# V loaded ahead, scale and router chains in parts, V split on GpSimd: a clustered attention feeding two MLP stages

## The chip, the cores and the metric

The kernel runs on one core of a Trainium2 chip (trn2). The metric is the device time of one execution in microseconds (us). An execution is one launch that computes the whole reference. The engines are TensorE (PE, with PEld for its weight loads), VectorE (DVE), ScalarE (ACT), GpSimd (POOL) and SyncE (SP), whose queue issues most DMAs. Each engine works through its own queue in order.

## What is computed

Attention with a cluster mask, then a mixture of experts with one expert per token, then a gated MLP:

```python
# q, k, v: (2, 8, 768, 64); centroids: (8, 16, 64)
q_assign = argmax(q_n . c_n); k_assign = argmax(k_n . c_n)   # nearest of 16 centroids
scores = scale * (q @ k^T), -1e9 where q_assign != k_assign
attn = exp(scores - max); attn /= sum
x = (attn @ v), heads side by side                            # (1536, 512)
e_idx = argmax(x @ w_gate)                                    # one of 8 experts
out[mask_e] = gate_w * eom * (relu(x[mask_e] @ w1[e]) @ w2[e])   # w1 512x1024
h = out @ w_in; return (h * sigmoid(h)) @ w_out               # 512x2048, 2048x512
```

All inputs are f32 and the result is f32.

## The kernel before

**Attention** takes the first 320 us or so. It goes through 2 batches x 8 heads in 8 pairs of heads, numbered 0 to 7; a pair has 12 steps, one for each 128-row tile of each of its two heads, 96 steps in all. In step i the loop `run` writes, in this order: the scores of step i+1 on TensorE (`qk_mm`, L367 and L369), the softmax of step i (`soft`: on VectorE the minimum L388, since the scores are held negated, on ScalarE the exp L390 and a cast to f16 L399), the transposed probabilities of step i-1, and the product with V (`pv`, L458 to L460) for a step that lies some 7 back.

The probabilities are kept as two f16 parts, a high one and what is left over. Transposing them goes one of two ways. For two steps in every six, which `onpe` picks, TensorE transposes the f32 (L414), ScalarE copies the high part (L420) and VectorE subtracts the low part (L425). For the others the high part comes from ScalarE (L399) or, in steps 4, 5 and 8 of a pair, from VectorE (L433); GpSimd subtracts the low part (L434) and a DMA on SP's queue transposes two steps at once (L438). `due` says from which step on a product may run.

**V** is used as two f16 parts as well, scaled by a power of two per head. `load_v` is a generator: it loads the V of a batch (768 rows x 8 heads, two DMAs of 768 KB, L118), takes the largest absolute value in four reductions (L123), and then turns it on TensorE, computes the scale on 8x8 tiles on VectorE (L128 to L135), spreads it with a matmul (L137) and copies it (L139). `split_v` makes the two parts of one head, `vh` and `vl` (L151, L152), twice per pair. The pool `att_v` of V has one buffer, so the second V (`vt` of batch 1) can be loaded only when the last head of batch 0 has been split.

**What sets the order.** `plan` makes for each pair a list of small pieces of work with a rank r (step in the pair, -1 being the step before it): the loads, transposes and masks of the next pairs, the splits, and for pairs 0 and 3 the parts of `load_v`. `run` takes from the list what is due in each step. Beside it runs at most one part per step of the router's generator `rg` (`pair`, for the gate logits of a pair of heads, and after the last pair of a batch `route`, the whole chain of expert choice, ranks and slots L713 to L747 and six scatters L757 of the rows into expert order). At the end of the attention part every instruction gets a dependency on its predecessor on the same engine, so the order written is the order run there.

**The experts** start with a read of the scattered rows back (`xt<-xst`) and TensorE's transposes (`etp`, L890) at about 340 us, with weights loaded ahead on SP's queue; then comes the gated MLP. TensorE is nearly always busy from there to the end.

## Time and profile before

| | us |
|---|---|
| Median of 3 runs | 868.56 (866.24 to 875.82) |
| The profiled execution | 866.39 |
| Span of its trace | 864.5 |
| Attention, first exp of pair 0 to last exp | 25.19 to 311.00 |
| Tail to the first expert | 311.00 to 340.00 |
| TensorE busy over the span | 753.1 (87%) |
| VectorE busy | 531.9 (62%) |
| ScalarE busy | 416.6 (48%) |
| GpSimd busy | 293.5 (34%) |

The rows further down come from one execution. A row of the windows gives for a stretch its length, then for each engine the busy time and the number of instructions, TensorE's granted clock (1.00 is 2.4 GHz, 0.50 is 1.2 GHz), the mean share of the 16 DMA engines and the rate moved. A row of the timeline gives start, duration, engine, line, operation, output<-input with their shapes, the number of operations in the row, and in brackets how long the engine had stood idle before it and what ended that. A row on a line gives the number of its instructions, their shortest, median and longest duration in ns, and where in the span they lie.

### The profile page before, as it was taken

The numbers are of one execution on the slowest core, as the hardware profiler recorded it, in microseconds if no ns is written. First come the engines' busy times: TensorE is split into PE (matmuls) and PEld (weight loads), VectorE is DVE, ScalarE is ACT, GpSimd is POOL, SyncE is SP. The second block draws the span as 40 slices with busy tenths as digits, with TensorE's granted clock in tenths as the row PEclk, the third lists the DMA queues.
The fourth block names the chain that finished last, engine by engine and source line by source line (L and its number), as shares of the span: only waits on it lengthen the run. The fifth ranks groups of instructions, "written<-read, shape, count | busy, mean of one in ns | idle before, by whom it ended". The sixth has DMA issues, their size and how long they took to land.

```text
span 864.5 us, 14020 instructions
## 1 busy us (share of the span) xinstructions
PE 753.1 (87%) x5404; PEld 639.3 (74%) x5404; DVE 531.9 (62%) x933; ACT 416.6 (48%) x657; POOL 293.5 (34%) x225
## 2 busy tenths in 40 slices
PE   5859897698899873999999999879799999999994
PEld 4649876597788762987887897657588788878883
DVE  6687886868989867366654778599933322232221
ACT  3747775466677644465444655456522322222211
POOL 1665563436744305654342546254400000000000
PEclk9658998579899995999999999979999999999998
DMA  4399899576877737587664874565400100010001
GB/s 149 69 221 208 172 167 244 108 151 121 206 137 126 152 102 268 193 274 237 232 221 131 281 256 129 199 227 174 144 1 0 50 1 1 0 49 1 0 1 52
DMA packets 138856, 117.88 MB, mean 136 GB/s; under 512 B 103927, under 2 KB 110071, under 8 KB 138784
## 3 DMA queue, kind: packets, MB, share of 16 engines
q1 hardware_dynamic: 134832, 107.85, 46.5%
q0 software_dynamic: 3952, 9.08, 3.7%
q8 instruction: 44, 0.72, 0.3%
q14 instruction: 28, 0.23, 0.1%
HBM read 71.67 MB, written 18.45 MB: 104 GB/s over the span
## 4 chain that ended last, share of the span: by engine, by line
PE 33%; DVE 8%; issue 4%; DMA 4%; ACT 1%; POOL 0%; ACTq 0%; SPq 0%; DVEq 0%; POOLq 0%
PE op L1131 13%; PE hp L1143 12%; PE yp L950 4%; DVE stage L1076 2%; PE hp L933 2%; PE hr L915 2%; DVE stage L1075 2%; DMA x<-ys,f 1%; DVE stage L1077 1%; DMA stage<-in_moe_w 1%; DMA stage<-in_moe_w_in 1%; DVE GL L837 1%; DMA out_x<-os 0%; DVE w L837 0%; DVE sg L1151 0%
## 5 line engine op out<-in xcount | busy, mean ns | idle before, releaser
L837 POOL TENSOR_TENSOR w<-stage,w 128x512 fp32r<-128x512 f32 (+1 forms) x54 | 102.7, 1909 | 110.9 <-ACT w L832 101.6
L434 POOL TENSOR_TENSOR p<-p,p 128x768 f16<-128x768 f32 x62 | 105.1, 1706 | 98.8 <-ACT p L390 38.4
L1143 PE MATMUL hp<-XH,w 128*128 128x512 f32 x384 | 126.5, 403 | 8.6 <-DVE sg L1151 7.5
L832 ACT ACTIVATE w<-stage 128x1024 fp32r<-128x1024 f32 (+1 forms) x104 | 96.4, 940 | 57.9 <-DVE stage L1077 25.9
L390 ACT ACTIVATE p<-sp,m 128x768 f32<-128x768 f32 x96 | 86.4, 900 | 59.9 <-DVE m L388 55.4
L1131 PE MATMUL op<-w,GH 128*128 128x512 f32 x384 | 112.0, 397 | 0.0
L1151 DVE TENSOR_TENSOR sg<-hp,sg 128x512 f32<-128x512 f32 x48 | 33.1, 689 | 118.9 <-ACT sg L1150 118.9
L388 DVE TENSOR_REDUCE m<-sp 128x1 f32<-128x768 f32 x96 | 90.8, 951 | 22.8 <-PE sp L369 16.9
L933 PEld LDWEIGHTS hp<-X,w 128*128 128x128 f32 x672 | 87.2, 192 | 12.7 <-DVE HL L936 9.2
L933 PE MATMUL hp<-X,w 128*128 128x256 f32 x672 | 90.9, 285 | 5.7 <-DVE HL L936 5.5
L1143 PEld LDWEIGHTS hp<-XH,w 128*128 128x128 f32 x384 | 73.5, 192 | 28.1 <-DVE sg L1151 9.7
L1150 ACT ACTIVATE sg<-hp 128x512 f32<-128x512 f32 x48 | 28.5, 594 | 119.8 <-PE hp L1143 118.7
L1131 PEld LDWEIGHTS op<-w,GH 128*128 128x128 f32 x384 | 73.0, 190 | 17.2
L837 DVE TENSOR_TENSOR w<-stage,w 128x1024 fp32r<-128x1024 f32 x50 | 69.7, 1403 | 25.6 <-ACT w L832 25.3
L458 PE MATMUL o<-vh,pt 128*128 128x66 f16 x576 | 68.9, 204 | 16.5 <-DVE xb L467 11.1
L1143 PE MATMUL hp<-XL,w 128*128 128x512 f32 x192 | 77.5, 403 | 2.7 <-DVE XL L837 2.7
L367 PE MATMUL sp<-KA,QA 128*128 128x384 f32 x192 | 66.7, 432 | 13.7 <-ACT p L390 13.1
L458 PEld LDWEIGHTS <-pt 128*128 128x128 f16 x576 | 56.7, 103 | 20.7 <-issue 10.1
L1131 PE MATMUL op<-w,GL 128*128 128x512 f32 x192 | 67.1, 397 | 1.9 <-DVE GL L837 1.8
L459 PE MATMUL o<-vl,pt 128*128 128x64 f16 x576 | 68.2, 200 | 0.0
L460 PE MATMUL o<-vh,pt 128*128 128x66 f16 x576 | 67.9, 201 | 0.0
L950 PE MATMUL yp<-w,HH 128*128 128x512 f32 x224 | 63.4, 398 | 0.6 <-ACT HH L935 0.6
(205 smaller groups left out, 1442.4 us busy)
## 6 DMA issues: line engine op xcount, KB each, us to landing
stage<-in_moe_w SPq DMA_DIRECT2D x72, 512.0 KB, 4.7
stage<-in_moe_w_in SPq DMA_DIRECT2D x16, 512.0 KB, 4.7
stage<-in_moe_w_out SPq DMA_DIRECT2D x16, 512.0 KB, 3.5
xst<-z SPq DMA_DIRECT2D x16, 258.0 KB, 3.5
xt<-xst SPq DMA_DIRECT2D x7, 516.0 KB, 3.9
vt<-in_v SPq DMA_DIRECT2D x4, 768.0 KB, 7.1
xt<-x SPq DMA_DIRECT2D x6, 512.0 KB, 5.2
out_x<-os SPq DMA_DIRECT2D x12, 256.0 KB, 2.5
```

The lines of the kernel that those rows point to most:

```text
L388: st['min'] = nc.vector.tensor_reduce(m, sv, axis=AX.XY, op=ALU.min).ins
L390: st['exp'] = nc.scalar.activation(p32, sv, AF.Exp, bias=m, scale=-1.0).ins
L434: s.nc.gpsimd.tensor_sub(p16[:, 1], p32, p16[:, 0])
L458: nc.tensor.matmul(o[:, t, 0:D + 2], lhsT=pt[:, 0, kt], rhs=vh[:, kt], start=kt == 0, stop=False)
L459: nc.tensor.matmul(o[:, t, 0:D], lhsT=pt[:, 0, kt], rhs=vl[:, kt], start=False, stop=False)
L460: nc.tensor.matmul(o[:, t, 0:D + 2], lhsT=pt[:, 1, kt], rhs=vh[:, kt], start=False, stop=kt == NT - 1)
L832: s.nc.scalar.activation(hi, src, AF.Copy)
L837: (eng or s.nc.vector).tensor_sub(lo, src, hi)
L933: nc.tensor.matmul(hp, lhsT=W1[k][w][:, f * 128:(f + 1) * 128], rhs=x[:, k, :N], start=n == 0, stop=n == 11)
L950: nc.tensor.matmul(yp, lhsT=h[:, f, i * 128:(i + 1) * 128], rhs=w, start=n == 0, stop=n == 23)
L1131: nc.tensor.matmul(op[i], lhsT=g[:, i * 128:(i + 1) * 128], rhs=w, start=f == 0 and m == 0, stop=f == 15 and m == 2)
L1143: nc.tensor.matmul(hp, lhsT=I[k, f // 8][w][:, fs], rhs=x[:, k], start=n == 0, stop=n == 11)
```

## The change

Buffers: the pool of V goes from one buffer to two; the pool of masks goes from two to one and that of the f16 probabilities (`p16`) from four to three.

V of batch 1 is loaded in pair 1 at rank 3 instead of in pair 3 at rank 1. Its maxima stand in pairs 1 and 2, two in each; the transpose, VectorE's scale chain, the matmul and the copy are now four parts, at ranks 4, 5 and 6 of pair 3. The parts for V of batch 0 are spread the same way in pair 0.

The split is three GpSimd operations: the scaling in place, a cast, a subtraction.

`route` yields between its pieces, so that the chain is a part per step, and one scatter is a part; parts marked 'free' may also run in steps whose transposes are on TensorE.

The last twelve steps all have their transposes on TensorE (before, the last eight), their products may come three steps after and up to three in one step.

```diff
-        s.mkp = P('att_mk', 2)
+        s.mkp = P('att_mk', 1)
-        s.p16 = P('att_p16', 4)
+        s.p16 = P('att_p16', 3)
-        s.vp = P('att_v', 1)
+        s.vp = P('att_v', 2)
...
         nc.tensor.transpose(pb[0:8, 0:128], am, s.ident)
+        yield
         g = s.sm.tile([8, 1], F32, tag='vg', name='vg')
...
         nc.vector.tensor_scalar(dg[:, 0], s.ident[0:8, 0:8], rg, None, op0=ALU.mult)
+        yield
         pb2 = s.T('vps2')
         nc.tensor.matmul(pb2[:, 0:16], lhsT=s.one8, rhs=dg.rearrange('p a h -> p (a h)'), start=True, stop=True)
+        yield
...
-        nc.vector.tensor_scalar(vh[:, :, 0:D], src, sc[:, 0, h:h + 1], None, op0=ALU.mult)
-        nc.vector.scalar_tensor_tensor(vl, src, sc[:, 0, h:h + 1], vh[:, :, 0:D], op0=ALU.mult, op1=ALU.subtract)
+        nc.gpsimd.tensor_scalar(src, src, sc[:, 0, h:h + 1], None, op0=ALU.mult)
+        nc.gpsimd.tensor_copy(vh[:, :, 0:D], src)
+        nc.gpsimd.tensor_sub(vl, src, vh[:, :, 0:D])
...
-            for r in (4, 5, 6, 7, 8, 8):
+            for r in (3, 4, 4, 5, 6, 7, 8, 8):
                 add(r, nx(vg))
...
-        if pi == 3:
+        if pi == 1:
             s.v1 = s.load_v(1)
-            for r in (1, 4, 5, 6, 7, 9, 9):
-                add(r, nx(s.v1))
+        for r in {1: (3, 6, 10), 2: (6, 10), 3: (4, 5, 6, 6)}.get(pi, ()):
+            add(r, nx(s.v1))
...
-        return (g % 3 == 0 and g >= 6) or g >= n - 4
+        return (g % 3 == 0 and g >= 6) or g >= n - 6
...
-            for k in range(2):
+            for k in range(3 if i >= n - 12 else 2):
                 if done < min(n, i + 1) and i >= s.due(steps[done]):
...
-                if rg and (k == 0 or (i - base) % 12 == 9 and i < n - 12) and not (1 <= i < n + 1 and i < n - 9 and s.onpe(steps[i - 1])) and next(rg[0], 1):
-                    rg.pop(0)
+                if rg and (k == 0 or (i - base) % 12 == 9 and i < n - 12) and (free or not (1 <= i < n - 12 and s.onpe(steps[i - 1]))):
+                    x = next(rg[0], 0)
+                    free = x == 'free'
+                    if x == 0:
+                        rg.pop(0)
...
-            return i + 3 if i >= len(s.steps) - 8 else i + 7
+            return i + 3 if i >= len(s.steps) - 12 else i + 7
...
-            s.route(b, att, g)
+            for x in s.route(b, att, g):
+                if not last:
+                    yield x
...
         nc.scalar.activation(ex, d, AF.Exp)
+        yield
         rk = att.T('rk')[:, :n * E9].rearrange('p (t e) -> p t e', t=n)
...
             nc.tensor.matmul(rk[:, lo:], lhsT=s.ones, rhs=o.unsqueeze(1).to_broadcast([128, n - lo, E9]), start=False, stop=i == len(prev) - 1)
+        yield
         nc.vector.tensor_tensor(d2, lg[:, :, E:2 * E], oh, op=ALU.mult)
...
         nc.scalar.activation(ev, ev, AF.Exp)
+        yield
...
             nc.vector.memset(o0, 0.0)
+        yield 'free'
         nc.vector.reduce_sum(sl, e3, axis=AX.X)
...
         for t in g:
+            yield 'free'
             s.scatter(s.xst, s.slot[:, b * NT + t:b * NT + t + 1], xb[:, t], E * CAP)
```

Three places show what moves. The first is SP's queue in pair 3 before, where the load of the second V (`vt`) stood among transposes, zero fills (`xst<-z`) and the copies of key rows:

```order
L438 DMA_TRANSPOSE pt<-p_1739 128x24x128
L1180 DMA xst<-z 128x516
L165 DMA qld_1877<-in_q 128x2x384
L165 DMA kld_1878<-in_k 128x2x384
L294 DMA KB<-KA 64x768
L438 DMA_TRANSPOSE pt<-p_1835 128x24x128
L1180 DMA xst<-z 128x516
L118 DMA vt_2005<-in_v 128x4x384 x2
L294 DMA KB<-KA 64x768
```

and now, in pair 1:

```order
L169 DMA qld_714<-in_q 128x2x384
L169 DMA kld_715<-in_k 128x2x384
L298 DMA KB<-KA 64x768
L442 DMA_TRANSPOSE pt<-p_652 128x24x128
L1195 DMA xst<-z 128x516
L118 DMA vt_970<-in_v 128x4x384 x2
L298 DMA KB<-KA 64x768
L442 DMA_TRANSPOSE pt<-p_922 128x24x128
```

The load holds the same place between transposes, two pairs earlier.

The second is GpSimd's queue where pair 2 begins, with the subtractions of the probabilities (`p_`) and the copies of query rows (`QB<-QA`); before:

```order
L434 TENSOR_TENSOR p_1270<-p_1268,p_1270 128x768
L149 MEMSET vh 128x6x2
L294 DMA QB<-QA 64x768
L434 TENSOR_TENSOR p_1270<-p_1308,p_1270 128x768
L149 MEMSET vh 128x6x2
L294 DMA QB<-QA 64x768
L434 TENSOR_TENSOR p_1483<-p_1481,p_1483 128x768
```

and now:

```order
L438 TENSOR_TENSOR p_1279<-p_1277,p_1279 128x768
L152 MEMSET vh 128x6x2
L154 TENSOR_SCALAR vt_339<-vt_339,vsc_597 128x384
L155 CAST vh<-vt_339 128x6x64
L156 TENSOR_TENSOR vl<-vt_339,vh 128x384
L298 DMA QB<-QA 64x768
L438 TENSOR_TENSOR p_1279<-p_1318,p_1279 128x768
L152 MEMSET vh 128x6x2
L154 TENSOR_SCALAR vt_339<-vt_339,vsc_597 128x384
L155 CAST vh<-vt_339 128x6x64
L156 TENSOR_TENSOR vl<-vt_339,vh 128x384
L298 DMA QB<-QA 64x768
```

Each of the two splits now stands ahead of a copy of query rows, and the first also ahead of the second subtraction of a pair of steps. VectorE's rows L151 and L152 at the same place are gone.

The third is VectorE's queue at the turn from pair 4 to pair 5, where the router chain of batch 0 begins with the maximum of the logits (`r_mx<-lacc`); before, from the minimum of one step to that of the next (the chain's later rows left out by stopping here):

```order
L688 TENSOR_TENSOR lacc_107<-lacc_107,lg 128x96
L713 TENSOR_REDUCE r_mx<-lacc_107 128x6
L714 TENSOR_TENSOR r_d<-lacc_107,r_mx 128x48
L715 SCALAR_TENSOR_TENSOR r_eq<-r_d,rev_85 128x48
L716 TENSOR_REDUCE r_mx<-r_eq 128x6
L717 TENSOR_TENSOR moe_oh<-r_eq,r_mx 128x6x8
L724 TENSOR_TENSOR r_d_3078<-lacc_107,moe_oh 128x48
L725 TENSOR_REDUCE r_ev<-r_d_3078 128x6
L726 TENSOR_SCALAR r_ev<-r_ev 128x6
L732 TENSOR_TENSOR r_e_3079<-rk,moe_oh 128x48
```

and now:

```order
L696 TENSOR_TENSOR lacc_107<-lacc_107,lg 128x96
L723 TENSOR_REDUCE r_mx<-lacc_107 128x6
L724 TENSOR_TENSOR r_d<-lacc_107,r_mx 128x48
L725 SCALAR_TENSOR_TENSOR r_eq<-r_d,rev_85 128x48
L726 TENSOR_REDUCE r_mx<-r_eq 128x6
L727 TENSOR_TENSOR moe_oh<-r_eq,r_mx 128x6x8
L392 TENSOR_REDUCE m<-sp 128x1 x2
L469 TENSOR_SCALAR rs<-o,vsc_2252 128x6
L470 RECIPROCAL rs<-rs 128x6
L471 TENSOR_TENSOR xb_67<-o,rs 128x6x64
```

After its first five operations two minima (`m<-sp`) come; the rest follows in three further places, five to eleven rows apart.

## Rows read from the trace of the kernel before

**Rows 1.** Windows by pair of heads, pairs 0 to 7, then the tail

```profile
25.19:68.26 43.07, 29.65 (x190) 25.36 (x189) 32.18 (x51) 26.70 (x38) 27.07 (x21) 0.62 0.78 161
68.26:98.39 30.13, 28.90 (x383) 26.40 (x383) 25.68 (x49) 23.73 (x40) 18.39 (x14) 0.99 0.86 176
98.39:130.91 32.52, 28.77 (x363) 26.20 (x361) 28.05 (x51) 23.95 (x40) 18.65 (x14) 0.95 0.98 186
130.91:184.57 53.66, 39.47 (x362) 35.67 (x360) 36.64 (x63) 24.66 (x40) 18.19 (x15) 0.66 0.78 173
184.57:219.61 35.04, 31.11 (x393) 28.32 (x393) 29.50 (x70) 24.29 (x42) 19.30 (x16) 0.94 0.71 141
219.61:252.71 33.10, 28.57 (x340) 25.90 (x339) 29.76 (x51) 23.74 (x39) 23.96 (x20) 0.90 0.73 156
252.71:282.63 29.92, 27.03 (x368) 24.33 (x367) 27.43 (x51) 21.33 (x34) 14.34 (x11) 1.00 0.76 138
282.63:311.00 28.37, 23.08 (x302) 20.75 (x298) 22.16 (x37) 18.81 (x32) 5.49 (x6) 0.94 0.65 156
311.00:340.00 29.00, 11.62 (x207) 10.65 (x207) 21.79 (x76) 12.05 (x19) 8.48 (x9) 0.69 0.47 163
```

**Rows 2.** Timeline of VectorE in pair 3

```profile
149.44 0.95 DVE L123 TENSOR_REDUCE vam<-vt 128x2 f32<-128x768 f32 x1 [6.61 <-DMA vt<-in_v]
...
170.30 1.49 DVE L135 TENSOR_SCALAR vdg<-ident,vrg 8x8 f32<-8x8 f32 x1
```

**Rows 3.** Timeline of ScalarE, exps at seven places

```profile
87.96 0.90 ACT L390 ACTIVATE p<-sp,m 128x768 f32<-128x768 f32 x1 [1.28 <-DVE m L388]
...
102.02 0.90 ACT L390 ACTIVATE p<-sp,m 128x768 f32<-128x768 f32 x1 [1.48 <-DVE m L388]
...
152.42 0.90 ACT L390 ACTIVATE p<-sp,m 128x768 f32<-128x768 f32 x1 [8.03 <-DVE m L388]
...
167.16 0.89 ACT L390 ACTIVATE p<-sp,m 128x768 f32<-128x768 f32 x1
...
175.30 0.89 ACT L390 ACTIVATE p<-sp,m 128x768 f32<-128x768 f32 x1
...
219.61 0.90 ACT L390 ACTIVATE p<-sp,m 128x768 f32<-128x768 f32 x1 [2.87 <-DVE m L388]
...
286.16 0.90 ACT L390 ACTIVATE p<-sp,m 128x768 f32<-128x768 f32 x1 [2.63 <-DVE m L388]
```

**Rows 4.** Windows of 5 us, one in pair 3

```profile
180.00:185.00 5.00, 5.00 (x35) 4.69 (x35) 1.90 (x3) 1.80 (x4) 0.65 (x2) 0.50 0.08 28
```

**Rows 5.** Timeline of VectorE at the router chain of batch 0

```profile
212.58 0.20 DVE L713 TENSOR_REDUCE r_mx<-lacc 128x6 f32<-128x48 f32 x1
...
218.60 0.92 DVE L388 TENSOR_REDUCE m<-sp 128x1 f32<-128x768 f32 x1
```

**Rows 6.** Lines L152 and L433 on VectorE

```profile
L152 DVE SCALAR_TENSOR_TENSOR vl<-vt,vsc,vh x16: 617/1882/2502, 52.7 to 283.3; 128x384 f16<-128x384 f32 x16
...
L433 DVE CAST p<-p x21: 549/551/3822, 36.9 to 277.0; 128x768 f16<-128x768 f32 x21
```

**Rows 7.** Lines L434 and L229 on GpSimd

```profile
L434 POOL TENSOR_TENSOR p<-p,p x62: 1627/1650/2032, 30.2 to 293.0; 128x768 f16<-128x768 f32 x62
...
L229 POOL CAST QB<-QA x2: 817/818/819, 8.6 to 13.9; 64x768 fp32r<-64x768 f32 x2
```

**Rows 8.** Timeline of GpSimd at two places

```profile
105.76 1.64 POOL L434 TENSOR_TENSOR p<-p,p 128x768 f16<-128x768 f32 x1 [4.39 <-issue]
...
229.25 5.23 POOL L434 TENSOR_TENSOR p<-p,p 128x768 f16<-128x768 f32 x3
```

**Rows 9.** Timeline of SP, and DMA issues (KB, median us to landing)

```profile
96.35 3.63 SPq L438 DMA_TRANSPOSE pt<-p  x1
...
pt<-p SPq DMA_TRANSPOSE x31, 6.7
```

**Rows 10.** Waits of TensorE: total, times, longest, from 335 on

```profile
PE etp L890 <- DMA xt<-xst: 12.9, 1, 12.9
```

## What the change is predicted to do

> **What bounds the kernel now.** I read the windows by head pair first [rows 1]: each row is one pair, 12 steps of one 128-row tile of one head (the last two rows are the last pair and the tail up to the first expert). The reader should compare TensorE's busy time with the length. In an undisturbed pair, such as 252.71:282.63, TensorE is busy 27.03 of 29.92 us at full clock, and VectorE 27.43: the two run neck and neck and everything else is under 22. So a step costs 2.5 us, and TensorE is the floor. One row stands out: 130.91:184.57 takes 53.66 us where its neighbours take 32.52 and 35.04. There TensorE is granted 0.66 of its clock.
>
> I then looked at what the engines do in that pair. On VectorE [rows 2] the first max of the second V waits 6.61 us for the load; the minimum of the next scores is queued behind it, so that the exp at 152.42 has waited 8.03 us [rows 3]. A second hole lies at 168 to 172: the V scale chain ends with a 1.49 us operation on 8x8 elements [rows 2], TensorE stands in its queue for it, and the exps at 167.16 and 175.30 lie 8.14 us apart [rows 3]. The holes bring a third loss: after them TensorE is busy for all of 180:185 at clock 0.50 (1.2 GHz) [rows 4], so the pair loses time even where it no longer waits.
>
> Smaller holes have the same form, a block on VectorE ahead of the next minimum. At 212.58 the router chain runs as one piece of some 20 operations until the minimum at 218.60 [rows 5], and its exp has waited 2.87 [rows 3]. At a pair's boundary the V split's second operation takes 1.88 us in the median against 0.62 at its fastest [rows 6], and exps wait 1.48 and 2.63 [rows 3]. VectorE's cast shows the same stretch, 0.55 to 3.82 [rows 6]: the 3.82 lies under three subtractions on GpSimd in a row [rows 8], so I read these as VectorE held up by a GpSimd operation in progress.
>
> **Part by part.**
>
> *V loaded ahead.* The second V gets its own buffer, so its load no longer waits for the last reader of the first and is issued two pairs earlier. The maxima stand 3 and more steps behind it, then in the next pair. This takes the 8.03 hole away and leaves VectorE four maxima in other places. In pair 1 the load costs something. That pair moves 176 GB/s at a DMA share of 0.86 [rows 1]; two loads of 768 KB are 1.57 MB, 8.9 us at that rate, while the free 14% of 30.13 us give 4.2. So the cost is between 0 (hidden: the next first use is seven steps after a transpose) and 4.7 us; I take 1.5, nearer to hidden, since only the transposes compete with it.
>
> *Scale chain in parts.* Its operations stay, but TensorE's two matmuls come one and two steps after what they read. The second hole (8.14 less a normal 2.5, 5.6 us) goes; the cover is the step of other work put between. If the cover fails, it costs at most those 5.6.
>
> With both holes gone TensorE has no reason here to fall to the low clock. The pair should then take what the ordinary ones do. Pairs 1, 2, 4, 5 and 6 take 29.92 to 35.04, and I take 31.0, at the lower side, because VectorE also loses the split: 53.66 - 31.0 = **22.7 gained** (bounds 18.6, if it goes like its slower neighbour, and 24.8, if it reaches the 28.90 that TensorE is busy in pair 1).
>
> *Router chain in parts.* Its work on VectorE is the same, but no longer in one piece: the stretch from 212.58 to 218.60 [rows 5] breaks into four of at most some 1.5 us, each after a minimum. Pair 4 goes from 35.04 to 31.0: **4.0** (bounds 2.9, the one exp's wait, and 6.0, the block). The six scatters move from one row ahead of the subtractions to places between them; pair 5's 33.10 holds the 3.82 cast that came of that row [rows 6, 8]. Against it GpSimd has 23.96 us there already. I take 31.0: **2.1** (bounds -3 and +4.2).
>
> *V split on GpSimd.* VectorE loses two operations a head, of which the second alone takes 1.88 us in the median [rows 6], 3.8 a pair; of that only what delays an exp counts (1.48 in one boundary, 2.63 in another [rows 3]). GpSimd gets three. Two of one input, 384 elements: its cast of 768 takes 0.82 [rows 7], so 0.41 to 0.82 each; one of two inputs: a subtraction of 768 takes 1.65 [rows 7], so 0.83 to 1.65. That is 1.65 to 3.3 a head; I take 2.2, near the halves. At a boundary GpSimd sits idle 4.39 before its work at 105.76 [rows 8], which covers one pair's 4.4, and the transpose that its last subtraction feeds isn't issued for some time after (SP is in order). Gains: pair 2 1.0, pair 1 1.0 (which with the 1.5 above leaves a **loss of 0.5**), pair 6 nothing, since it is at TensorE's floor. So pair 2 **1.0**. Pair 0 has these splits in its second half, but there the transposes on SP set the end; **1.0** (bounds 0 and 3).
>
> The Trainium skill (GPSIMD Engine Reference, 4.1 Engine selection) speaks against this edit: elementwise work belongs on VectorE, and GpSimd takes about twice as long for two inputs and about as long for one. No run here shows one operation on both engines; by that rule alone the two-input part goes from the fastest 0.62 to 1.24 and the rest stays, an estimate of 16 x 0.62 = 10 us more engine time; were it all on the path, the time would be 842.
>
> *Buffers.* The price is paid with one mask buffer less and a p16 buffer less (4 to 3). A buffer is now written again 8 steps later, 8 x 2.51 = 20.1 us; the one whose exp stands at 87.96 [rows 3] is read by the transpose issued at 96.35, which lands 6.7 later [rows 9], 15.1 us after the exp. So 5.0 us are spare: cost 0, and a rival below.
>
> *Last pair and tail.* One pair of steps goes to TensorE instead of a DMA transpose, and four of nine V products that stood after the last scores move ahead. TensorE's tail row is 11.62 us for 207 matmuls [rows 1]; four products are 72 of them, 4.0 us at that mean, the upper bound (lower 0, if the exps end it anyway); I take 2. With the exp at 286.16, which waits 2.63 [rows 3], worth 2 of it: **4.0** (bounds 1 and 6). What follows hangs on it: the first expert waits 12.9 us for the gathered rows [rows 10], whose chain begins at the last V product, and that chain is unchanged. The loads of expert weights change places on SP by a few steps; I take 0 (bounds -3 and +3).
>
> **The sum.** 22.7 + 4.0 + 2.1 + 1.0 - 0.5 + 1.0 + 4.0 = 34.3. The profiled execution took 866.39 (span 864.5), 2.2 under the median of the runs shown. 866.39 - 34.3 = **832.1**; I say 832.
>
> **Rivals.**
>
> A. *Everything reaches TensorE's floor.* Relieved of splits and blocks, pairs 1 to 6 all take the 28.90 that TensorE is busy in pair 1: 214.37 - 173.4 = 41.0, with 5 for the ends 46: **820**. For it: VectorE is the second bound in every row. Against: pair 6 has few stalls and still takes 29.92.
>
> B. *GpSimd becomes the queue.* If the splits' 4.4 a pair lie on the path in seven pairs, 31 of the 34 go: **863**. It decides where GpSimd has less than 4.4 free: pair 5 (23.96 + 4.4 of 31). The other rows have 18 to 19, so I give it little.
>
> C. *The hole moves.* The load costs its whole 4.7 in pair 1, and the chain's small operations still take over a microsecond each next to GpSimd's work, now more of it, so that TensorE waits 5.6 again and falls to its low clock for some steps (another 3): 832 + 3.2 + 5.6 + 3 = **844**.
>
> D. *GpSimd holds VectorE up.* Each of 16 splits stops one VectorE operation for a half-size subtraction, 0.85: 13.6 us, **846**. For it: the 3.82 cast. Against: what is stretched in the rows are the cast and the split, the split is leaving, and the casts come at steps 4, 5 and 8 of a pair, away from its boundary, except in pair 0. The Trainium skill (SBUF — State Buffer, Who interferes with whom) has the mechanism: VectorE shares one pair of ports with GpSimd as an exclusive lock, taken by its casts and by operations with two inputs in SBUF, never by reduces. The stretched cast and split [rows 6] agree with it.
>
> E. *Slower: three p16 buffers are too few.* ACT, in order, stops at a cast whose buffer is still being transposed, and all exps behind it. It decides when a transpose lands more than 5.0 us later than above; to lose all 34.3 and 9 more over 31 transposes each must be 1.4 beyond that, 6.4 late: **875**. For it: splits and scatters push subtractions back, and the V load lies ahead of transposes on SP. Against: that is one or two transposes a pair, not all.
>
> **How the numbers follow.** My forecast 0.70, A 0.10, C 0.07, B 0.05, D 0.05, E 0.03. The range 819 to 847 takes in A, C and D and leaves out B, E and some of the forecast's own spread. About 1% (8.7 us) is what a measurement of this kernel can tell from no change, given 866.24 to 875.82 in three runs. Faster by more: the forecast, A, C and D, 0.92. Within 1%: B, 0.05. Slower: E, 0.03.
>
> **What would show it.** Right: exps in pair 3 about 2.6 apart, no VectorE wait for the V load, no TensorE wait for the 8x8 operations, the clock near 1.00 where 180:185 had 0.50, no gap at the router step; GpSimd's three new operations near 2.2 us together with its idle time gone at the boundaries. Wrong: TensorE waiting for DMA transposes (B), exps waiting for a cast (E), casts stretched in every pair (D), a long pair 1 (C). My sum fails first if pair 3 keeps a hole, since two thirds of it lie there.

## The result and the profile after

The changed kernel takes 862.98 us (median of 20 runs, 858.08 to 868.78) where the kernel before takes 871.84 (20 runs). The ratio is 0.9908, 95% interval 0.9883 to 0.9934: 0.9% faster, some 8 us. The forecast was 832 with a range of 819 to 847. A second comparison on another chip gave 0.9884 (0.9822 to 0.9946). Some executions of a kernel fall in a slower state; the ratios leave them out, while the medians hold all. The profiled execution has a span of 856.0, against 864.5 before.

The windows by pair of heads, with the columns of [rows 1], pairs 1 to 7:

```profile
67.92:101.85 33.93, 29.72 (x379) 26.95 (x379) 24.86 (x48) 24.10 (x40) 24.28 (x22) 0.95 1.07 223
101.85:132.43 30.58, 28.57 (x365) 25.98 (x365) 24.75 (x48) 23.75 (x39) 21.14 (x18) 0.98 0.96 179
132.43:171.28 38.85, 31.80 (x366) 29.24 (x364) 26.41 (x53) 23.87 (x40) 22.96 (x21) 0.82 0.88 155
171.28:208.97 37.69, 30.18 (x384) 27.76 (x383) 25.77 (x52) 23.98 (x40) 24.16 (x22) 0.86 0.86 147
208.97:246.07 37.10, 29.24 (x330) 26.43 (x329) 26.68 (x61) 23.83 (x38) 25.08 (x23) 0.86 0.70 158
246.07:277.80 31.73, 29.76 (x368) 27.06 (x366) 25.29 (x47) 21.61 (x36) 21.85 (x21) 0.95 0.74 140
277.80:307.00 29.20, 25.89 (x391) 24.09 (x390) 21.46 (x39) 18.51 (x34) 7.43 (x10) 1.00 0.55 139
```

Set against the lengths in [rows 1], us:

| stretch | forecast | measured | 
|---|---|---|
| pair 0 | -1.0 | -0.1 |
| pair 1 | +0.5 | +3.8 |
| pair 2 | -1.0 | -1.9 |
| pair 3 | -22.7 | -14.8 |
| pair 4 | -4.0 | +2.7 |
| pair 5 | -2.1 | +4.0 |
| pair 6 | 0 | +1.8 |
| pair 7 and tail | -4.0 | +0.8 and -1.6 |
| ahead of pair 0; experts and MLP | 0 | -0.2; -2.9 |
| sum | -34.3 | -8.4 |

(The tail is the time from the last exp to the first of the experts' transposes, 311.0 to 339.4 before and 307.0 to 333.8 after. The sum differs from that of the spans, 8.5, by rounding.) VectorE was relieved as foreseen: its busy time is lower in each of these rows, by 3 us on average in pairs 2 and 4 to 6. But the time didn't follow. The granted clock, for which the forecast was near 1.00 in pair 3, is 0.82 there (0.66 before) and 0.86 in pairs 4 and 5 (0.94 and 0.90 before). TensorE's waits say what came instead. Waits of TensorE over the attention part, after (total, times, longest):

```profile
PE o L462 <- DMA pt<-p: 15.9, 3, 7.3
...
PE sp L373 <- DMA KB<-mk: 5.4, 2, 3.4
```

and before:

```profile
PE o L458 <- DMA pt<-p: 5.2, 2, 3.7
```

The product with V waits for a DMA transpose three times as long as before. The longest two stand at the same place of their pairs, step 6 of pair 3 (6.8 us) and of pair 4 (7.3 us). SP's queue ahead of the first (`qld`, `kld`: loads of queries and keys; `KB<-KA`: a copy of key rows), and TensorE's wait:

```profile
135.22 0.44 SPq L169 DMA_DIRECT2D qld<-in_q  x1
135.70 1.47 SPq L169 DMA_DIRECT2D kld<-in_k  x1
137.26 0.86 SPq L298 DMA_DIRECT2D KB<-KA  x1
138.23 6.83 SPq L442 DMA_TRANSPOSE pt<-p  x1
...
146.38 6.97 SPq L442 DMA_TRANSPOSE pt<-p  x1
```

```profile
151.81 0.24 PE L462 MATMUL o<-vh,pt 128*128 128x66 f16 x1 [6.84 <-DMA pt<-p]
```

The transposes of the kernel before took 6.7 us in the median [rows 9] and 10.6 at the longest. Now their longest is 13.7 (shortest, median, longest):

```profile
DMA to landing us min/median/max: 5.4/6.8/13.7
```

The median is the same, so the transposes are not slow as such; the one issued at 138.23, behind two loads and a copy, took 13.5, and the 13.7 is the one that pair 4 waits for. And the DMA engines are full at these places. Windows of 5 us in the changed kernel, ahead of pair 0, at the two long waits and behind the first of them; the last three numbers are the granted clock, the DMA share and GB/s:

```profile
15.00:20.00 5.00, 2.67 (x24) 2.53 (x24) 4.26 (x14) 0.15 (x1) 0.00 (x0) 0.77 0.00 2
20.00:25.00 5.00, 4.72 (x22) 2.90 (x20) 3.40 (x7) 1.35 (x4) 0.00 (x0) 0.50 0.00 0
...
145.00:150.00 5.00, 0.00 (x0) 0.00 (x0) 4.37 (x7) 1.07 (x3) 2.91 (x3) 0.74 1.22 141
150.00:155.00 5.00, 3.19 (x27) 2.72 (x28) 0.02 (x1) 0.70 (x1) 2.92 (x2) 0.50 1.16 246
...
160.00:165.00 5.00, 4.87 (x61) 4.23 (x61) 2.34 (x5) 2.75 (x5) 0.00 (x0) 0.90 0.01 3
...
185.00:190.00 5.00, 0.00 (x0) 0.00 (x0) 0.57 (x2) 1.20 (x2) 4.96 (x3) 0.50 1.23 129
```

While TensorE waits, the share stands at 1.16 to 1.23 (in these rows it goes above 1), and the clock falls to 0.50; ten microseconds later the engines move next to nothing, and before pair 0 nothing at all. The kernel before has full stretches too: in its pair 2 every window from 100 to 125 shows 1.05 to 1.25, and there TensorE waits only 1.5 us for a transpose. So a full share goes with the long waits, but doesn't make one by itself.

### The profile page after: what moved, and what is told of

The parts are those of the page before. It is cut to its first block, busy times and chain, and to the rows that moved or that the text cites. A ratio compares the mean times of both kernels' runs of the same rounds, so it can differ in the third digit from the quotient of the medians.

```text
span 856.0 us, 14041 instructions
## 1 busy us (share of the span) xinstructions
PE 749.6 (88%) x5416; PEld 636.4 (74%) x5416; DVE 501.9 (59%) x905; ACT 415.2 (48%) x659; POOL 328.6 (38%) x271
## 4 chain that ended last, share of the span: by engine, by line
PE 33%; DMA 5%; issue 5%; DVE 4%; POOL 2%; ACT 1%; ACTq 0%; POOLq 0%; DVEq 0%
PE op L1146 13%; PE hp L1158 13%; PE yp L965 3%; DMA x<-ys,f 3%; PE hp L948 2%; POOL w L852 2%; PE hr L930 2%; DMA stage<-in_moe_w_out 1%; DVE stage L1091 1%; DVE stage L1092 1%; DVE stage L1090 1%; DMA stage<-in_moe_w_in 1%; DMA stage<-in_moe_w 1%; DMA out_x<-os 0%; ACT w L847 0%
## 5 line engine op out<-in xcount | busy, mean ns | idle before, releaser
L1158 PE MATMUL hp<-XH,w 128*128 128x512 f32 x384 | 128.5, 406 | 6.8 <-DVE sg L1166 5.6
L438 POOL TENSOR_TENSOR p<-p,p 128x768 f16<-128x768 f32 x60 | 98.4, 1650 | 72.7 <-DVE p L437 42.3
L462 PE MATMUL o<-vh,pt 128*128 128x66 f16 x576 | 67.7, 202 | 22.2 <-DMA pt<-p 15.9
L464 PE MATMUL o<-vh,pt 128*128 128x66 f16 x576 | 66.9, 199 | 0.0
```

Source lines behind the costliest of these rows:

```text
L438: s.nc.gpsimd.tensor_sub(p16[:, 1], p32, p16[:, 0])
L462: nc.tensor.matmul(o[:, t, 0:D + 2], lhsT=pt[:, 0, kt], rhs=vh[:, kt], start=kt == 0, stop=False)
L464: nc.tensor.matmul(o[:, t, 0:D + 2], lhsT=pt[:, 1, kt], rhs=vh[:, kt], start=False, stop=kt == NT - 1)
L1158: nc.tensor.matmul(hp, lhsT=I[k, f // 8][w][:, fs], rhs=x[:, k], start=n == 0, stop=n == 11)
```

## The experiments

Two theories stood at the start (their letters are new and not those of the prediction's rivals). **S**: the V split on GpSimd delays the subtractions, and with them the transposes. **D**: the DMA engines are the limit of pairs 1 to 4 once the holes of V are gone, wherever the split is. GpSimd's rows speak for S at first sight. At the boundary to pair 3:

```profile
131.83 1.25 POOL L154 TENSOR_SCALAR vt<-vt,vsc 128x384 f32<-128x384 f32 x1
133.15 0.51 POOL L155 CAST vh<-vt 128x384 f16<-128x384 f32 x1
133.74 0.89 POOL L156 TENSOR_TENSOR vl<-vt,vh 128x384 f16<-128x384 f32 x1
134.57 0.58 POOL L298 DMA_DIRECT2D QB<-QA  x1
```

A head costs 2.74 us from 131.83 to 134.57, where 2.2 was taken; the scaling in place takes 1.25, not 0.41 to 0.82. The times of all runs, each against the kernel before on its chip (which took 871 to 879 us on the chips used, so the ratios are to be compared; e1 to e4 ran on one chip, e5 to e12 on a second, c13 and e14 on a third):

| run | us | ratio, interval |
|---|---|---|
| changed kernel | 862.98 | 0.9908 (0.9883 to 0.9934) |
| the same, other chip (c13) | 864.26 | 0.9884 (0.9822 to 0.9946) |
| e1, split on VectorE | 867.18 | 0.9959 (0.9926 to 0.9991) |
| e2, rank tile in one part | 862.26 | 0.9912 (0.9880 to 0.9945) |
| e3, split in steps 7 and 8 | 860.47 | 0.9873 (0.9811 to 0.9935) |
| e4, V load in quiet steps | 858.50 | 0.9857 (0.9813 to 0.9902) |
| e5, fills at the start | 854.29 | 0.9752 (0.9700 to 0.9804) |
| e6, last pair as before | 869.39 | 0.9912 (0.9874 to 0.9951) |
| e7, router in one part | 859.96 | 0.9831 (0.9772 to 0.9889) |
| e8, fills and V load at the start | 851.06 | 0.9696 (0.9637 to 0.9755) |
| e9, e8 + e7 + e6, split in steps 7 and 8 | 847.52 | 0.9644 (0.9598 to 0.9689) |
| e10, e8 + e7 + e6, split on VectorE | 862.91 | 0.9816 (0.9770 to 0.9862) |
| e11, before, fills at the start | 871.81 | 0.9885 (0.9833 to 0.9937) |
| e12, e8 + e7 + e6, split as changed | 847.86 | 0.9641 (0.9592 to 0.9689) |
| e14, fills paired | 866.31 | 0.9924 (0.9885 to 0.9963) |

**e1: the split back on VectorE.**

```diff
-        nc.gpsimd.tensor_scalar(src, src, sc[:, 0, h:h + 1], None, op0=ALU.mult)
-        nc.gpsimd.tensor_copy(vh[:, :, 0:D], src)
-        nc.gpsimd.tensor_sub(vl, src, vh[:, :, 0:D])
+        nc.vector.tensor_scalar(vh[:, :, 0:D], src, sc[:, 0, h:h + 1], None, op0=ALU.mult)
+        nc.vector.scalar_tensor_tensor(vl, src, sc[:, 0, h:h + 1], vh[:, :, 0:D], op0=ALU.mult, op1=ALU.subtract)
```

> The changed kernel with the V split put back on VectorE (L151, L152 of before), all else as changed. In the changed kernel TensorE waits 6.8 us in pair 3 and 7.3 us in pair 4 for a DMA transpose (15.9 in all), and its clock falls there. Theory S (the split on GpSimd, 2.8 us a head ahead of a subtraction and of the copy of query rows, makes the transposes late): these waits fall under 2 us in all, pairs 3 and 4 go from 38.9 and 37.7 to 33 to 35 us although VectorE has its boundary blocks back, and the total is about 6 us under the changed kernel, some 857. Rival D (the transposes are late because the faster pace after the removed VectorE blocks asks for them earlier, and because loads and copies share the DMA engines): VectorE's blocks come back and slow the pace too, so the waits shrink as well, but each boundary's first two steps cost 3.6 and 1.8 us again and the total stays within 3 us of the changed kernel, 860 to 866.

Waits of TensorE for transposes, and pair 1 as the columns of [rows 1]:

```profile
PE o L461 <- DMA pt<-p: 8.8, 5, 4.2
```

```profile
67.04:104.68 37.64, 30.45 (x380) 27.59 (x378) 27.76 (x51) 23.77 (x40) 19.31 (x16) 0.91 1.02 196
```

Pairs 3 and 4 fall to 33.2 and 34.0 as S says, but 8.8 us of waits stay, pair 1 grows to 37.6 with one step of 9.1, and the attention part ends at 305.4 against 307.0. The total is not lower: 867.18, some 10 us above what S says and 1 above the range of D. The waits are halved, and the longest that is left, 4.2, now lies in pair 1. S as the whole cause falls here; as a part of the waits in pairs 3 and 4 it stays open.

**e2: the rank tile in one part.** The division of the router leaves one PSUM tile, of three that all transposes share, waiting from the rank matmuls at 210.31 to its reading at 222.17. That was a third suspect, for pair 5 alone.

```diff
-        yield
         nc.vector.tensor_tensor(d2, lg[:, :, E:2 * E], oh, op=ALU.mult)
...
         nc.scalar.activation(ev, ev, AF.Exp)
-        yield
```

> The changed kernel with two of the router's yields taken out, so that the rank matmuls and the operations that read their PSUM tile stand in one part again. In the changed kernel this tile, one of three that all transposes share, is written at 210.3 and read at 222.2, and pair 5 has steps of 5.6, 4.7 and 5.5 us. Theory R (the held tile starves the transposes): pair 5 goes from 37.1 to 32 to 33 us and the total falls 4 to 5, to about 858. Rival (pair 5 is long because six scatters and two splits share GpSimd, and the clock fell for another reason): pair 5 stays at 36 to 38 and the total at 863.

The total is the same, 0.9912, and pair 5 takes 40.3 us, not 32 to 33. The tile is not what makes pair 5 long. But pair 6 takes 27.5 instead of 31.7, which e7 explains.

**e3: the split in steps 7 and 8 of the pair before.**

```diff
-        for h, r in enumerate((9, 10) if z else (-1, 0)):
-            add(r, sp(h))
+        if z:
+            for h, r in enumerate((9, 10)):
+                add(r, sp(h))
+        if pi == 1:
+            for h, r in enumerate((-1, 0)):
+                add(r, sp(h))
+        if 1 <= pi < len(pairs) - 1:
+            for h, r in enumerate((7, 8)):
+                add(r, sp(h, *pairs[pi + 1]))
```

> The changed kernel with the splits of pairs 2 to 7 written in steps 7 and 8 of the pair before, where GpSimd stands idle some 5 us before the next subtractions, instead of at the boundary. GpSimd's work is the same. Theory S: the subtractions and the copies of query rows at the boundary come 2.8 to 5.6 us earlier, TensorE's waits for DMA transposes in pairs 3 and 4 fall under 3 us in all, and those pairs take 31 to 33; total about 851, better than with the split on VectorE. Rival D (pace and DMA sharing): the waits stay above 8 us and the total at 860 or more.

```profile
PE o L469 <- DMA pt<-p: 11.9, 4, 4.0
```

11.9 us of waits stay where S expects under 3, and pair 3 takes 34.6. The ratio, 0.9873, can't be told from that of the changed kernel. S as the whole cause falls a second time. But pairs 3 and 4 take 34.6 and 34.2, as short as in e1 (38.9 and 37.7 in the changed kernel, 38.5 and 36.5 in its second execution), which speaks for a share of the split at the boundary in their waits, though single pairs vary by as much between executions; the gain is lost again in pair 6, which takes 37.7.

**e4: the V load in quiet steps.**

```diff
+            if b and g == 0:
+                yield
...
-        for r in {1: (3, 6, 10), 2: (6, 10), 3: (4, 5, 6, 6)}.get(pi, ()):
+        for r in {1: (9,), 2: (9, 10, 10), 3: (2, 3, 4, 5, 6, 6)}.get(pi, ()):
```

> The changed kernel with the two halves of the second V's load issued at step 9 of pairs 1 and 2, where the DMA engines are nearly idle (share 0.17 in the quiet stretch of pair 2), instead of both at step 3 of pair 1; the maxima follow later. In the changed kernel a transpose issued right behind the load holds SP's queue 9.4 us, the mask copies are issued 3.4 us later than before and TensorE waits 1.9 for one; pair 1 takes 33.9 against 30.1 before. Theory L (the load in front of the transposes costs this): pair 1 returns to 30 to 31 us and the total falls by 3, to 860. Rival (pair 1 is longer for the single mask buffer and the shorter p16): pair 1 stays at 33 to 34.

Pairs 1 and 2:

```profile
69.68:99.07 29.39, 28.17 (x382) 25.72 (x380) 23.03 (x46) 23.66 (x39) 22.70 (x20) 1.00 0.99 217
99.07:135.26 36.19, 30.29 (x371) 27.77 (x369) 25.22 (x49) 23.96 (x39) 23.94 (x21) 0.86 1.04 189
```

Pair 1 comes back to 29.4, as expected: without the load the 3.8 us are not lost. But the half that is now loaded at the end of pair 1 stands ahead of the transposes of pair 2, which takes 36.2 with one step of 8.3. TensorE's waits for transposes are 17.9 in all, no shorter than in the changed kernel. Bytes moved from a full stretch to the next full stretch give little: 0.9857, an interval that overlaps that of the changed kernel.

**e5: the zero fills at the start.** The 16 fills that stood behind transposes are issued while the DMA engines move nothing.

```diff
         next(vg)
+        for _ in range(16):
+            s.bgdma.pop(0)()
```

> The changed kernel with the 16 zero fills (xst<-z, 258 KB each) issued in a row behind the first V load, at the start, where the DMA engines move nothing from 15 to 35 us, instead of one behind each transpose of pairs 0 to 4. Theory D (after the two holes are gone the DMA engines are the limit of pairs 1 to 4: in pair 2 they are busy at a share of 0.94 to 1.15 for 20 of 30 us, and TensorE waits for transposes, 15.9 us in all): each of these pairs loses three fills, some 0.77 MB or 4 us of DMA time, the waits for transposes fall under 6 us in all and pairs 1, 3 and 4 lose 2 to 4 us each; total about 852. Rival S (the transposes are late at the source, because the subtractions on GpSimd are): the waits stay at 14 to 16 and the total at 860 to 863.

Pairs 1, 3 and 4, and TensorE's wait for transposes:

```profile
66.26:96.60 30.34, 28.25 (x382) 25.80 (x381) 24.75 (x48) 23.63 (x39) 23.23 (x21) 1.00 0.94 200
...
128.76:162.38 33.62, 30.71 (x366) 28.22 (x364) 26.32 (x53) 23.86 (x40) 22.96 (x21) 0.90 0.81 148
162.38:195.46 33.08, 29.75 (x384) 27.33 (x383) 25.77 (x52) 23.97 (x40) 24.17 (x22) 0.95 0.82 159
```

```profile
PE o L462 <- DMA pt<-p: 10.4, 4, 3.0
```

Pairs 1, 3 and 4 lose 3.6, 5.2 and 4.6 us, from 33.9, 38.9 and 37.7; no wait is longer than 3.0; TensorE's wait for mask copies (5.4 after) is 2.3. The ratio falls by 1.6 points. With the split exactly where the change put it, the transposes come in time for the most part. This is what D says, except that the waits end at 10.4 and not under 6. The changed kernel itself was not run on this chip; e7, run there with the fills in their old places, has 18.0 us of these waits and a pair 3 of 38.1, so the fall is not the chip's.

**e14: the same bytes in half as many issues.** e5 also frees SP's queue of 16 issues. This run leaves the bytes where they were and halves the issues.

```diff
-            att.bgdma = [lambda d=d, z=z: nc.sync.dma_start(d, z) for d, z in m.zeros()]
+            zs = [(m.xst[i * 256:(i + 1) * 256].rearrange('(t p) c -> p t c', p=128), m.z.unsqueeze(1).to_broadcast([128, 2, RW])) for i in range(E * CAP // 256)] + m.zeros()[16:]
+            att.bgdma = [lambda d=d, z=z: nc.sync.dma_start(d, z) for d, z in zs]
+            att.nth = 0
...
-                if s.bgdma:
+                s.nth += 1
+                if s.bgdma and (s.nth % 2 or s.nth > 16):
```

> The changed kernel with the 16 zero fills issued as 8 of twice the size, behind every second transpose: the same bytes in the same stretch, half the issues on SP's queue. Theory D1 (the DMA engines are what the transposes wait for): waits of TensorE for transposes stay at 13 to 18 us and the ratio at 0.988 to 0.994. Theory D2 (SP's queue is, which issues fills and transposes in order, 0.58 us a fill): the waits fall to about 10 as with the fills at the start, and the ratio to 0.98 or less.

```profile
PE o L463 <- DMA pt<-p: 24.0, 5, 8.9
```

The waits don't fall; they are 24.0, above even what D1 says, and the ratio is 0.9924. So it is not the number of issues (0.58 us each, as before, now for twice the bytes). With e5 this speaks for the bytes ahead of a transpose. Queue and engines are not wholly told apart by it, because a transpose holds SP's queue itself while it is issued, 3.6 to 9.4 us in the changed kernel.

**c13: the changed kernel again**, on another chip than its first comparison:

> The changed kernel itself, once more beside the kernel before on the same chip as the later runs, since the kernel before takes 871 us on one chip and 878 on another. If the chips differ only by a factor, the ratio is 0.988 to 0.993 as in its first comparison, and the runs with the fills at the start (0.975 and 0.970) stand 1.5 to 2% under it on their own chip. If the changed kernel gains more on this chip, its ratio is under 0.983 and the fills explain less.

0.9884, and 18.5 us of waits for transposes; one of them (6.2 us) makes a step of 8.8 in pair 2 that the first execution didn't have. This chip is not that of e5 to e12 either; e6 and e7 stand in for the changed kernel there. The waits fall on one pair or another from execution to execution; their sum is what stays. That also bounds the reading of any single pair in these runs to some 5 us.

**e6: the last pair as before.**

```diff
-        return (g % 3 == 0 and g >= 6) or g >= n - 6
+        return (g % 3 == 0 and g >= 6) or g >= n - 4
...
-            for k in range(3 if i >= n - 12 else 2):
+            for k in range(2):
...
-                if rg and (k == 0 or (i - base) % 12 == 9 and i < n - 12) and (free or not (1 <= i < n - 12 and s.onpe(steps[i - 1]))):
+                if rg and (k == 0 or (i - base) % 12 == 9 and i < n - 12) and (free or not (1 <= i < n - 9 and s.onpe(steps[i - 1]))):
...
-            return i + 3 if i >= len(s.steps) - 12 else i + 7
+            return i + 3 if i >= len(s.steps) - 8 else i + 7
```

> The changed kernel with the last pair and the tail as before: the last eight steps, not twelve, on TensorE, the lag of their products and the products per step as before. In the changed kernel two steps of pair 7 take 4.2 and 6.3 us, because three products run in one step ahead of the next scores and each waits for VectorE to empty the one output tile; the tail is 1.6 us shorter than before. Theory (what the tail gains is paid in pair 7): pair 7 falls by 0 to 3 us, the tail grows by 1.6, and the total stays within 2 us of the changed kernel. Rival (this part brings the 4 us that were forecast): the total rises by 4, to 867.

Undoing the part costs nothing: 0.9912, where the changed kernel has 0.9908 and 0.9884. What it does in pair 7 of the changed kernel is seen on TensorE, and on ScalarE behind it:

```profile
292.17 0.19 PE L462 MATMUL o<-vh,pt 128*128 128x66 f16 x1 [1.23 <-DVE xb L471]
...
297.03 0.19 PE L462 MATMUL o<-vh,pt 128*128 128x66 f16 x1 [1.08 <-DVE xb L471]
```

```profile
298.13 0.49 ACT L682 ACTIVATE xt<-xtp 128x384 f32<-128x384 f32 x1 [4.25 <-PE xtp L680]
```

Up to three products stand ahead of the next scores, each new group of them waits until VectorE has emptied the one output tile, and two steps take 4.2 and 6.3 us. In the runs with everything at the start, pair 7 takes 29.2 with this part (e8) and 25.8 without it (e12), while the tail takes 25.6 and 26.9 (from the last exp to the experts' first transposes): 3.4 lost for 1.3 won.

**e7: the router's chain in one part.**

```diff
-            for x in s.route(b, att, g):
-                if not last:
-                    yield x
+            for _ in s.route(b, att, g):
+                pass
```

> The changed kernel with the router's chain in one part again. Theory (divided, the chain costs in pair 5 what it gives at the step between pairs 4 and 5): that step takes 7 to 8 us again instead of 3.8, pair 5 goes from 37.1 to 33 or 34, and the total stays within 2 us of the changed kernel, 861 to 865. Rival (the division brings the 4 us that were forecast): the total rises to 867.

Pairs 4 to 6 in one window, this run, and then the changed kernel:

```profile
173.53:275.40 101.87, 87.39 (x1078) 79.14 (x1075) 74.86 (x159) 68.86 (x112) 71.17 (x64) 0.92 0.77 156
```

```profile
171.28:277.80 106.52, 89.18 (x1077) 81.26 (x1075) 77.74 (x159) 69.42 (x113) 71.10 (x64) 0.89 0.77 149
```

The router step takes 7.8 us again where the division had made it 3.8, as expected. But pairs 5 and 6 take 33.3 and 27.5 instead of 37.1 and 31.7. Divided, the chain loses 4.6 us over the three pairs more than it saves, and the ratio is 0.9831 against 0.9908 (0.9912 in e6 on the same chip, the intervals just touching): more than the 2 us that the theory had allowed. The runs e8 and e12 show the same: pairs 4 to 6 take 102.9 us with the divided chain and 97.7 with the chain in one part. One thing that differs between the runs is when the scatters are through. In the changed kernel the last stands between the subtractions of pair 6:

```profile
244.54 1.68 POOL L438 TENSOR_TENSOR p<-p,p 128x768 f16<-128x768 f32 x1
246.38 1.00 POOL L772 DMA_INDIRECT xst<-xb,slot  x1 [0.16 <-issue]
```

In e7 the last is issued at 220.46, early in pair 5, and in e2 at 238.51; both have a pair 6 of 27.5 us, as e9 and e12 have. In e3 it is issued 2.8 us into pair 6, which is the longest of all (37.7). That the late scatters cost pair 6 its 4 us fits all of these, but no run moved the scatters alone.

**e8: the fills and the second V's load at the start.**

```diff
         next(vg)
+        s.v1 = s.load_v(1)
+        next(s.v1)
+        for _ in range(16):
+            s.bgdma.pop(0)()
...
-        if pi == 1:
-            s.v1 = s.load_v(1)
-        for r in {1: (3, 6, 10), 2: (6, 10), 3: (4, 5, 6, 6)}.get(pi, ()):
+        for r in {1: (6, 10), 2: (6, 10), 3: (4, 5, 6, 6)}.get(pi, ()):
```

> The run with the fills at the start, and the load of the second V there too, behind the first V's. Theory D: the DMA engines get 1.57 MB less in pair 1 as well, which falls from 33.9 to 29 or 30 us; total 3 to 5 under the run with the fills alone, some 848. Rival L (4.1 and 1.6 MB ahead of pair 0 delay its loads, and pair 0 grows by 3 us or more): total no better than the changed kernel.

0.9696, whose interval overlaps that of e5. Pair 1 takes 30.3 as in e5: with the fills gone, the load in pair 1 is hidden. Pair 0 takes 41.3, so nothing is lost in front either (rival L falls).

**e9, e10, e12: everything together, with the split in three places.** All three have e8's start, e7's router and e6's last pair.

> Buffers, early V and scale chain as changed; the fills and the second V's load at the start; router chain in one part and last pair as before; splits on GpSimd in steps 7 and 8 of the pair before. Theory D (the DMA engines were the limit) with the router's and the tail's parts costing 4 to 5 and 1 us: pairs 1 to 4 take 30 to 34 us each with one 8 us step at the router, pairs 5 and 6 33 and 28, pair 7 26; ratio to the kernel before 0.958 to 0.968, the best so far. If the remaining waits for transposes (10.4 us with the fills at the start) come of the subtractions standing behind splits, they fall under 4 us here and pairs 2 to 4 reach 31; if not, they stay.

> As the run with the splits in steps 7 and 8, but with the V split on VectorE at the boundary as before. Theory S (with the DMA engines relieved, the split on GpSimd still delays the transposes): waits for transposes under 3 us in all, but VectorE's 1.9 to 2.5 us operations are back, so each boundary costs 2 to 3 us again; ratio 0.965 to 0.975. Rival (the split's place doesn't matter any more): same pairs and the same ratio as the other two to within 0.3%.

> As the run with the splits in steps 7 and 8, but with them on GpSimd at the boundary, as in the changed kernel. If the place matters with the DMA engines relieved, TensorE's waits for transposes are 8 to 10 us in all and pairs 2 to 4 take 2 us more each than with the splits in steps 7 and 8: ratio 0.965 to 0.972. If not, the two are the same within 0.3%.

The sums over the eight pairs, e12 (split on GpSimd at the boundary) and then e10 (on VectorE):

```profile
sum 263.50, PE 229.10 PEld 206.41 DVE 194.89 ACT 185.61 POOL 183.62; mean PE 28.64 PEld 25.80 DVE 24.36 ACT 23.20 POOL 22.95
```

```profile
sum 273.76, PE 231.91 PEld 209.02 DVE 228.99 ACT 187.30 POOL 144.93; mean PE 28.99 PEld 26.13 DVE 28.62 ACT 23.41 POOL 18.12
```

The split on GpSimd takes 34 us off VectorE and the eight pairs 10.3 us shorter; the ratios are 0.9641 and 0.9816, far apart. In which step GpSimd does it does not matter (0.9644 in steps 7 and 8). e10 gained less than either theory gave it (0.965 to 0.975, or the same as the others), and e12 a little more (0.965 to 0.972). So with the fills and the load out of the way the split is worth 1.7%; in the changed kernel it is worth some 0.5% (e1, the intervals overlapping). These two, at 0.964, beat both kernels: 3.6% under the kernel before. Waits of 8 to 10 us for transposes remain in them (8.1 in e9, 10.3 in e12, 7.4 in e10, with the split on VectorE), so neither the place of the split nor the fills account for those; what does is open.

**e11: the fills at the start of the kernel before.** The same four lines as e5, in the kernel before.

> The kernel before with nothing changed but the 16 fills, issued at the start. Theory D in its strict form (the DMA engines become the limit only once the V holes are gone; before, TensorE waited 5.2 us for transposes and its pairs 1 and 2 took 30.1 and 32.5): pair 0 loses some 2 us, pair 2 some 2, pair 3 keeps both holes (50 us or more), total 4 to 6 under the kernel before, ratio 0.993 to 0.996. Rival (the DMA engines were a limit all along, and the fills alone bring most of the gain): ratio 0.985 or less.

Pair 3 keeps both holes (51.5 us), the exps from first to last take 284.8 against 285.8, and the waits for transposes go from 5.2 to 1.5. The ratio is 0.9885, interval 0.9833 to 0.9937, between what the two theories expect and overlapping the strict one at its edge only. The trace gives the attention part 1 us, the timing some 5 to 15; no row here explains the rest, but the execution with the trace is the slowest of the six, and that of the kernel before among its fastest. What can be said: the same edit gives 0.9884 or 0.9908 to 0.9752 on the changed kernel and between 0.6 and 1.7% on the kernel before. The times don't show that the DMA engines became a limit only through the change; the waits speak for a larger part of it after (15.9 to 10.4) than before (5.2 to 1.5).

## Why the prediction was wrong, point by point

**What bounds the kernel: the step that failed.** The prediction read TensorE and VectorE off [rows 1], put everything else under 22 us, and gave TensorE's wait for transposes no term in its sum, so that pairs 3, 4 and 5 could fall to 31.0. The DMA share stands in the same rows: 0.86 and 0.98 in pairs 1 and 2, 0.78 in pair 3 although TensorE was idle for 14.2 us of it, and 0.76 of 29.92 us, 22.7, in the pair that was taken as undisturbed. The prediction used the 0.86 once, to price the V load, and not as a bound on the transposes that share the engines. Pair 3's 0.78 of 53.66 us is 41.9 us of DMA time. The V load's 8.9 us are at a share of 0.86, that is 7.7; without them 34.2 are left, and in 31.0 us they ask for a share of 1.10. No whole pair of the two kernels has that; the highest, 1.07, is pair 1 after, which grew longer. The changed kernel's pair 3 has 0.88 of 38.85 us, 34.2 again.

What the runs showed in its place: TensorE waits 15.9 us for transposes instead of 5.2, its clock falls behind these waits, and with the fills out of the way (e5) the waits are 10.4 and pairs 1, 3 and 4 take 13.4 us less. The division for pair 3 could have been made before the run. It would not have caught everything: pair 4's 0.71 of 35.04 us is 24.9, which fits 31.0 with ease, and yet this pair lost 7.3 us to one transpose while the share stood at 1.23. A mean over a pair hides such a stretch.

**Pair 3 (22.7 forecast, 14.8 measured).** The first hole is gone, and so is TensorE's wait for the 8x8 operations. The reason was right, the size was off by the transposes: e5, with the fills moved, gains 20.0 here (53.66 to 33.62), e8 18.2 and e12 17.8. The second hole is only halved. The chain still stands between two minima; VectorE and GpSimd at step 41, with the exps behind:

```profile
144.51 1.18 DVE L133 TENSOR_SCALAR vdg<-ident,vg 8x8 f32<-8x8 f32 x1
145.61 0.14 DVE L135 RECIPROCAL vrg<-vg 8x1 f32<-8x1 f32 x1
145.79 1.66 DVE L136 TENSOR_SCALAR vdg<-ident,vrg 8x8 f32<-8x8 f32 x1
...
154.98 0.17 DVE L142 COPY vsc<-vps 128x16 f32<-128x16 f32 x1 [5.55 <-PE vps L139]
```

```profile
144.02 1.65 POOL L438 TENSOR_TENSOR p<-p,p 128x768 f16<-128x768 f32 x1 [0.57 <-DVE p L437]
145.62 1.80 POOL L331 TENSOR_TENSOR nq<-qld,nq 128x768 fp32r<-128x768 f32 x1
```

```profile
149.06 0.90 ACT L394 ACTIVATE p<-sp,m 128x768 f32<-128x768 f32 x1 [3.93 <-DVE m L392]
...
156.79 0.90 ACT L394 ACTIVATE p<-sp,m 128x768 f32<-128x768 f32 x1 [6.10 <-DVE m L392]
```

The first exp waits 3.93 because the two 8x8 operations take 2.84 together; that step takes 5.5 to 5.6 us in every run with the divided scale chain. The second waits 6.10 because the copy of the scale stands ahead of the minimum and waits for a matmul that TensorE, stuck at its transpose, has not reached: a wait on one queue was passed to two others. Part of rival C was this.

**Pair 1 (0.5 forecast as a loss, 3.8 measured).** The value of 1.5 for the V load was too small. The bound of 4.7 lies above the loss only because it set 8.9 us at a share of 0.86 against free time at full share; with 7.7 it would be 3.5. e4, which moves the load, and e5, which moves the fills, both bring the pair back (29.4, 30.3), so the loss needs the two together. The value was chosen "nearer to hidden" because only the transposes were to compete. But TensorE's wait for a DMA in this pair is for a copy of masked key rows (`KB<-mk`, 1.9 us), and for no transpose.

**Pairs 4 and 5 (4.0 and 2.1 forecast, 2.7 and 4.0 lost).** At the router step the mechanism was right: 8.4 became 3.8. Pair 4 then lost 7.3 us at step 54 to a transpose, and pairs 5 and 6 what e7 shows. The prediction counted the division as nearly free because its work on VectorE is the same; it bounded the cost of the scatters in pair 5 (3 us; 4.0 were lost) and named none in pair 6, into which they now reach.

**The split (1.0 forecast in each of pairs 0 to 2, and part of the 31.0 in others).** GpSimd had the room: the changed kernel is no slower with the split there than on VectorE (e1), so the prediction's rival B (GpSimd as the queue) is not what took the time, although its sign, TensorE waiting for transposes, came, and e1 and e3 leave it open whether the split has a part in that. Rival D (GpSimd holding VectorE up) shows in the 8x8 operations, but not in the casts: these take 0.55 in the median as before and 2.54 at the longest, against 3.82. The gain was under-sized for a kernel with the fills and the load out of the way: 4 us by e1, 10 to 15 by e10 and e12.

**The Trainium skill's rule** (GPSIMD Engine Reference, 4.1 Engine selection), to keep elementwise work off GpSimd, holds in its direction for the price of the operations here (2.74 us a head against 2.29 on VectorE, medians of 0.41 and 1.88) and not for the time (0.9641 with the split on GpSimd, 0.9816 on VectorE): VectorE was shared with the minima that every exp waits for, and GpSimd had gaps.

**Buffers and tail.** ScalarE waited 2.0 us for a free p16 buffer in all and VectorE 0.5: rival E's mechanism is there, at a price of 2.5 us and not 43. The late transposes that E asks for did come (13.5 and 13.7 us), but they told at TensorE's product and not at ScalarE's cast. The last pair and the tail were forecast to bring 4.0 and bring 0.8 together (1.6 won in the tail, 0.8 lost in pair 7); undone in e6, the time stays the same.

**The range.** The sum was of independent gains, each stall replaced by the length of an undisturbed pair. All rivals kept that, too. None asked what the DMA engines allow when several pairs get faster at once, so no case stood between 847 and B's 863, and that B's 863 is the time measured is luck: it was added up from splits on the path in seven pairs.

## What to carry to other kernels

Before a hole is priced at its whole length, divide the work that each resource has in that stretch, the DMA engines among them, by the length that you forecast; a share of 0.78 in a stretch that is to shrink to 0.6 of its length asks for 1.3, less what leaves the stretch. Divide by short windows too, since a mean over a stretch hides a full one. When a wait leaves one engine and the time does not follow, look for the same total of waits at other steps: a single pair tells little, the sum over the pairs tells which limit it is. Transfers with no deadline (zero fills, loads far ahead) belong where the DMA engines are idle, which the windows show at a glance; that gave as much as the change itself here, or more (0.9885 alone in e11; from 0.9908 and 0.9884 to 0.9696 on top of the change in e8).

## What the runs showed of the hardware

Three things had not been expected. A scaling of 128x384 f32 in place takes GpSimd 1.25 us, more than a subtraction of two inputs to f16 of the same size (0.89) and more than twice a cast (0.51). The Trainium skill (GPSIMD Engine Reference, 4.1 Engine selection) has one-input operations at about VectorE's rate; the cast may fit that against VectorE's 0.41 for the scaling of the same tile to f16 (fastest of L151), the scaling does not. No run here scales in place to f32 on VectorE.

VectorE's operations on 8x8 elements take 1.18 and 1.66 us when GpSimd is at work, against 0.22 at 44.35, where GpSimd stands idle, and they end when GpSimd's operation ends: 144.51 + 1.18 = 145.69 against 144.02 + 1.65 = 145.67, and 145.79 + 1.66 = 147.45 against 145.62 + 1.80 = 147.42. An operation of a few elements pays for what is left of one of GpSimd's. This agrees with the exclusive lock of the Trainium skill (SBUF — State Buffer, Who interferes with whom).

A DMA transpose takes 5.4 us to land at the least and 13.7 at the most in one execution, by what stands ahead of it; the most was 15.5 in the second execution of the same kernel, 10.6 in the kernel before, and 15.4 with fills of twice the size. Its issue holds SP's queue from 3.6 to 9.4 us.
